# Ten joined pairs of p1 and p2, a re-ordered step list and 124 unread matmuls in a fused recurrence and rational feed-forward kernel

## The chip, the cores and the metric

The kernel runs on one core of one Trainium2 chip. The metric is the device time of one execution in microseconds (us), lower is better; a comparison goes by the median of several executions. Five engines work from instruction queues of their own, each strictly in order: TensorE (PE, with its weight loads shown as PEld), VectorE (DVE), ScalarE (ACT), GpSimd (POOL) and SyncE (SP, which here only issues DMAs).

## The reference

For 4 batches and 8 heads a state of 48 x 48 is decayed per row by a gate and receives an outer product at each of 768 steps; the query reads it. The heads' outputs, put side by side, go through a feed-forward layer whose activation is a rational function.

```python
# B, H, S, D = 4, 8, 768, 48
f = 1.0 / (1.0 + np.exp(-f_logit))
for t in range(S):
    state = f[:, :, t, :, None] * state + np.einsum('bhd,bhe->bhde', k[:, :, t], v[:, :, t])
    y[:, :, t] = np.einsum('bhd,bhde->bhe', q[:, :, t], state)
x = y.transpose(0, 2, 1, 3).reshape(B * S, H * D)          # 3072 x 384
h = x @ w_in                                               # 384 x 2048
P = a[0] + a[1] * h + a[2] * h**2 + a[3] * h**3
Q = 1.0 + np.abs(b[0]) * np.abs(h) + np.abs(b[1]) * h**2
out = (P / (Q + 1e-06)) @ w_out                            # 2048 x 384
```

## The kernel before

The work is cut into 12 units of 256 tokens; unit n is chunk n // 4 of batch n % 4, so that the state of a batch passes from unit n to unit n + 4. Within a unit the recurrence is done in two blocks of 128 tokens, by the chunked form: logarithms of the gates are summed over time with triangular matrices, q and k are scaled with the exponentials of those sums, and the output is a masked product inside the block plus a read of the state that enters it.

Every operation is a *step*, a short name with a unit and ranges, and one long string, `ORDER`, lists all steps. A loop at the end of the kernel calls them in that order; nothing else sets the order, so each engine executes its own steps in the order of the list. The steps:

- loads: `ld n f|q|k` on SP, `ld n v` on POOL; `wi` and `wo` load pieces of the two weights on POOL, `ab_` the coefficients. A pair of numbers after a load, as in `ld 0 f 2 4`, limits it to some of the head pairs 0 to 4. Constants: `ci` (identity), `cu 0` and `cu 1` (the triangular matrices Ui and Us), `cm`, `cz`; `fa`, `fb`, `fr` derive coefficients.
- gates: `ef` and `ls` on ACT (exponential, logarithm), `cs` on PE (the sums), `A` on ACT (exponential of the sums; `A n 0` for q, `A n 1` for k).
- recurrence: `xa n x` scales q (x = 0) or k (x = 1), on DVE or, with `p`, on POOL; `T` transposes the scaled q and k on PE; `Te` takes the result out of PSUM, on ACT with `s`, else on DVE; `sc n g` are the products of q and k on PE, `mk n g` masks them on DVE; `ic` and `si` build the next state on PE, `st n j` scales it on DVE; `yb` and `yi` form the output y on PE; `ye` evicts it as x. `vm` copies parts of v.
- feed-forward: `h n m0 m1` multiplies x with pieces m0 to m1 of the 16 column blocks of w_in (12 matmuls for four pieces); `hy` evicts them on ACT; then over halves `0 8` and `8 16` or the whole `0 16`: `sq` or `sa` (square, on DVE or ACT), `ab` (absolute value), `p1` and `p2` (two linear factors of P), `pm` (p1 times the square), `zv` on DVE or `zd` as an accumulating DMA (the denominator), `rq` (its reciprocal, ACT), `tv` or `ta` (the numerator, on DVE or as a DMA), `gm` (their product, DVE). `o n j m0 m1` multiplies with w_out, `oe` evicts, `so` stores.
- `tab` loads the activation table of the logarithm (0) or of the reciprocal (1).

`@0` to `@3` name one of four PSUM slots of two banks that a step opens; the slot is free again when the step that reads it is done, for example `hy` for `h`, `mk` for `sc`, `A` for `cs`, `st` for `ic`. `!m5` on a step and `^m5` on a later one on another queue make the later one wait for the first. Buffers rotate: one T and one masked product, two scaled q and k, three each of f, k, q, v, g and z, four x and hy.

Of the kernel before, what the change touches and what calls it, by code (L numbers as in the profile page):

```python
# [34 lines left out]
ye 2 s; ab 1 0 8; sc 3 0 @3; cs 5 @2; A 4 0; ab 0 0 8 !m8; xa 4 0 2 4 p ^m8; mk 3 0; A 4 1; ic 3 @1; sa 1 8 16
h 2 8 12 @0; st 3 0; ld 5 k; sq 0 0 8; si 3 1; h 2 12 16 @3; hy 2 8 12; pm 0 0 8 !m7; zd 0 0 8; ld 5 q
xa 4 1 2 4 p ^m7; ls 6; sc 3 1 @0; st 3 1 !m6; A 5 1; ld 6 k; vm 3 ^m6; mk 3 1; h 2 4 8 @1; ld 5 v; hy 2 12 16
xa 4 1 0 2; ef 7; yi 3 1 @0; xa 4 0 0 2; yb 3 0 2; wo 12 16; p1 1 8 16; hy 2 4 8; T 4 @3; wo 8 12
pm 1 8 16 !m10; A 5 0; ic 4 @1; wo 4 8; xa 5 1 0 2 p ^m10; si 4 0; Te 4 s; yb 3 2 4; st 4 0 !m11; ye 3 !m9
xa 5 1 2 4 p ^m11; si 4 1; sc 4 1 @2; h 2 0 4 @3; ld 7 k; mk 4 1; vm 4 ^m9; tab 1; rq 0 0 16; wo 0 4  # L40
sc 4 0 @0; p2 0 0 8 !m13; xa 5 0 2 4 p ^m13; yb 4 2 4 @2; st 4 1 !m12; xa 5 0 0 2 p ^m12; mk 4 0; si 5 0 @1
yi 4 0; ic 5; st 5 0; yb 4 0 2; tv 0 0 8 !m14; si 5 1; hy 2 0 4; h 3 4 8 @0; ld 6 q; ld 6 v ^m14; st 5 1
gm 0 0 8; yi 4 1; h 3 8 12 @3; zd 1 0 8; tab 0; ls 7; p1 1 0 8; h 3 12 16 @1; ye 4 s; gm 0 8 16; hy 3 4 8
zv 1 8 16; T 5 @2; hy 3 12 16; cs 6 @0; p1 2 8 16; Te 5 s; vm 5 v; o 0 0 12 16 @1; p2 1 0 16; hy 3 8 12
o 0 1 12 16; A 6 0; sc 5 0 @2; ab 2 0 8; cs 7 @3; A 6 1; pm 1 0 8; o 0 0 8 12; ef 8; sc 5 1 @0
xa 6 1 0 2 !m15; A 7 0; xa 6 1 2 4 p ^m15; o 0 1 4 8; mk 5 0 !m18; A 7 1; o 0 0 4 8; xa 7 1 0 2 p ^m18
sa 2 0 16; mk 5 1; h 3 0 4 @3; ta 1 8 16; sq 3 8 16; h 4 4 8 @2; p1 2 0 8; h 4 0 4 @0; tv 1 0 8; ls 8
zd 2 0 8; o 0 1 8 12; xa 6 0 2 4; hy 3 0 4; p2 2 0 8; o 0 1 0 4; hy 4 0 4; ab 2 8 16; yi 5 1 @3; yi 5 0
o 0 0 0 4; p2 2 8 16; hy 4 4 8; zd 2 8 16; ld 7 v ^m13; yb 5 0 2; pm 2 0 16 !m16; oe 0 0 2 s; yb 5 2 4
# [571 lines left out]
```

## Time and profile before

| | |
|---|---|
| median of three runs | 212.93 us (211.46 to 214.59) |
| profiled execution | 210.19 us, of which the span of instructions is 208.5 us |
| mean granted TensorE clock | 0.988 |
| busy: PE, DVE, ACT, POOL | 191.0, 187.0, 186.1, 77.8 us |
| matmuls, weight loads | 2894, 2894 |
| DMA | 43.15 MB, 207 GB/s in the mean |

The busy times are shares of the span; a row of a timeline gives the start, the duration, the engine, the line of the code, the operation with its tiles and shapes, and in brackets how long the engine stood idle before it and what ended that. A group of matmuls ends later than its last one starts by about a fifth of a microsecond.

### The profile page before, as it was taken

How to read it: one execution, taken by the hardware profiler on the slowest of the kernel's cores; microseconds unless marked ns; L12 is line 12 of the kernel's file. 1: busy time of each engine (PE TensorE's matmuls, PEld its weight loads, DVE VectorE, ACT ScalarE, POOL GpSimd, SP SyncE). 2: the span in 40 equal slices, each digit the busy share in tenths (PEclk: the TensorE clock that was granted, in tenths of full speed). 3: DMA queues.
4: the chain of work that ended last, by engine and by line, in shares of the span. 5: the costliest groups of instructions: out<-in, count | busy, mean ns of one | idle time of the engine just before them, and what ended most of it. 6: DMA issues, size and time to landing. Idle time of an engine off the chain costs nothing.

```text
span 208.5 us, 6605 instructions
## 1 busy us (share of the span) xinstructions
PE 191.0 (92%) x2894; PEld 139.4 (67%) x2894; DVE 187.0 (90%) x235; ACT 186.1 (89%) x172; POOL 77.8 (37%) x99
## 2 busy tenths in 40 slices
...
PEclk9999699999999999999999999999999999999998
...
GB/s 98 287 300 186 271 220 253 186 220 233 168 206 202 85 176 152 249 267 265 208 222 252 250 199 229 209 200 210 185 191 163 214 211 195 193 190 183 238 146 167
DMA packets 61820, 43.15 MB, mean 207 GB/s; under 512 B 51424, under 2 KB 56544, under 8 KB 61792
## 3 DMA queue, kind: packets, MB, share of 16 engines
...
q14 instruction: 6, 0.05, 0.1%
...
## 4 chain that ended last, share of the span: by engine, by line
PE 75%; DVE 10%; DMA 6%; SPq 4%; issue 2%; ACT 1%; DVEq 0%
PE op L549 31%; PE hp L469 26%; PE y L389 6%; SPq L209 4%; PE cs L304 3%; DMA v<-in_v_dram 3%; PE tp L345 3%; PE sc L368 2%; DMA q<-in_q_dram 2%; DVE scm L376 2%; DVE g L528 2%; PE sv L434 2%; DVE state L459 1%; PE sv L444 1%; DVE qkp L331 1%
## 5 line engine op out<-in xcount | busy, mean ns | idle before, releaser
L549 PE MATMUL op<-w_out_sb,g 128*128 128x384 bf16 x384 | 68.6, 326 | 0.0
L469 PE MATMUL hp<-x,w_in_sb 128*128 128x256 bf16 x576 | 68.0, 273 | 0.3 <-DVE state L459 0.3
L469 PEld LDWEIGHTS <-w_in_sb 128*128 128x128 bf16 x576 | 55.4, 98 | 9.4 <-issue 0.7
L549 PEld LDWEIGHTS <-g 128*128 128x128 bf16 x384 | 35.8, 98 | 22.6 <-DVE g L540 0.4
L481 ACT CAST hy<-hp 128x1024 bf16<-128x1024 f32 x48 | 47.8, 1027 | 2.6 <-PE hp L469 2.3
L508 ACT ACTIVATE z<-z 128x4096 bf16<-128x4096 bf16 (+1 forms) x16 | 44.5, 2780 | 1.1 <-DVE z L499 1.1
L540 DVE TENSOR_TENSOR g<-g,z 128x2048 bf16<-128x2048 bf16 (+2 forms) x24 | 28.9, 1218 | 1.1 <-issue 0.6
L503 POOL DMA_DIRECT2D z<-h x20 | 20.6, 1077 | 24.7 <-ACT h L490 17.0
L528 DVE TENSOR_TENSOR g<-g,h 128x2048 bf16<-128x2048 bf16 (+1 forms) x21 | 28.8, 1373 | 0.1
L376 DVE TENSOR_TENSOR scm<-sc,mask 128x1024 bf16<-128x1024 f32 x24 | 28.8, 1216 | 0.0
L490 ACT ACTIVATE h<-hy 128x2048 bf16<-128x2048 bf16 (+1 forms) x13 | 26.8, 2073 | 0.0
L326 ACT ACTIVATE A<-cs 128x768 f32<-128x768 f32 (+3 forms) x26 | 19.0, 779 | 6.5 <-PE cs L312 6.5
L532 POOL DMA_DIRECT2D g<-hy x15 | 13.8, 943 | 28.3 <-DVE g L528 9.3
L304 PE MATMUL cs<-lsp,Ui 128*128 128x384 bf16 (+1 forms) x39 | 12.0, 371 | 10.1 <-ACT lsp L294 8.7
L518 DVE TENSOR_SCALAR g<-hy,a_sb 128x2048 bf16<-128x2048 bf16 (+1 forms) x23 | 18.9, 829 | 1.4 <-ACT hy L481 1.4
L331 POOL TENSOR_TENSOR qkp<-k,A 128x384 bf16<-128x384 f32 x11 | 11.0, 1025 | 23.6 <-DVE g L540 10.4
L523 DVE TENSOR_SCALAR hy<-hy,a_sb 128x2048 bf16<-128x2048 bf16 (+1 forms) x20 | 18.3, 915 | 0.4
L209 POOL DMA_DIRECT2D v<-in_v_dram x12 | 12.1, 1012 | 15.7 <-DVE qkp L331 8.3
L494 DVE TENSOR_SCALAR z<-hy 128x2048 uint16<-128x2048 uint16 (+1 forms) x21 | 15.8, 764 | 0.0
L459 DVE TENSOR_TENSOR state<-sv,A 128x384 bf16<-128x384 f32 x20 | 11.0, 552 | 4.5 <-PE sv L444 2.4
L389 PE MATMUL y<-scm,v 64*32 64x128 bf16 x384 | 14.0, 218 | 0.8 <-DVE scm L376 0.7
L331 POOL TENSOR_TENSOR qkp<-q,A 128x384 bf16<-128x384 f32 x10 | 10.0, 1010 | 11.5 <-ACT A L326 5.5
...
## 6 DMA issues: line engine op xcount, KB each, us to landing
...
v<-in_v_dram POOLq DMA_DIRECT2D x12, 192.0 KB, 7.7
out_dram<-f SPq DMA_DIRECT2D x12, 192.0 KB, 3.9
out_dram<-osb SPq DMA_DIRECT2D x10, 192.0 KB, 6.4
```

Source lines behind the costliest of these rows:

```text
L209: return eng.dma_start(out=s[what][:, hh].rearrange("p h i d -> p h (i d)"), in_=src[s["b"], hh, t0:t0 + NT, :].rearrange("h (p i) d -> p ...
L331: i = (nc.gpsimd if eng == "p" else nc.vector).tensor_mul(s["qk"][:, x, :, hh, 0:D], s["qk"[x]][:, hh].rearrange("p h i d -> p i h d"), s[ ...
L376: return nc.vector.tensor_mul(t, s["sc", g].rearrange("s r a i t -> s (r a) (i t)"), mb)
L389: nc.tensor.matmul(s["y"][32 * a:32 * a + 32, j, kk * C:kk * C + C].rearrange("e (i t) -> e i t", i=2), lhsT, rhs, start=(j, a) not in s[" ...
L469: nc.tensor.matmul(t[:, m - m0, :].rearrange("f (j t) -> f j t", j=UB), w_in_sb[:, kk, m * P:(m + 1) * P], s["x"][:, :, kk, :], start=(kk ...
L481: nc.scalar.copy(fl(big(s, "hy"), m0, m1), fl(s["hp", m0], 0, m1 - m0))
L490: return nc.scalar.activation(fl(big(s, "h2"), m0, m1), fl(big(s, "hy"), m0, m1), AF.Square)
L503: return nc.gpsimd.dma_start(out=fl(big(s, "z"), m0, m1), in_=fl(big(s, "h2"), m0, m1), accum_op=ALU.add)
L508: return nc.scalar.add_instruction(mybir.InstActivation(name=nc.get_next_instruction_name(), func=AF.Reciprocal, ins=[nc.scalar.lower_ap(f ...
L528: return nc.vector.tensor_mul(fl(big(s, "g"), m0, m1), fl(big(s, "g"), m0, m1), fl(big(s, "h2"), m0, m1))
L540: return nc.vector.tensor_mul(fl(big(s, "g"), m0, m1), fl(big(s, "g"), m0, m1), fl(big(s, "z"), m0, m1))
L549: nc.tensor.matmul(s["op", g][:, j, 0:DM], big(s, "g")[:, m, C * j:C * j + C], w_out_sb[:, m, :], start=(s["on", j] == 1), stop=(s["on", j ...
```

## The change

Three things change, all in `ORDER` but for one new step.

- A new step `dn n w sl` opens a PSUM slot and issues n matmuls of Us with w times 64 columns of itself; nothing reads them. `dn 62 1` stands ahead of `cs 0` and `dn 62 2` between `cs 0` and `cs 1`.
- Where both halves of a unit went through `p1` or `p2` in two instructions, more of them now go through one. Joined now: `p1` of units 2, 3, 4 and 10 (6 stays so) and `p2` of units 2, 4 and 8 (7 and 10 stay so); taken apart: `p2` of units 1 and 3. In the same way `pm` of 6 and 7 and `gm` of 2 and 6 are joined, `pm` of 2 and 5, `gm` of 4 and 7, `ab` of 6, 7 and 9, and the DVE products `xa 8 0` and `xa 10 1` are taken apart, and `rq` of 6 and 7 on ACT.
- All other steps are the same, in another order: mostly a few places off. `Te 0 0 2` moves from ACT to DVE, `xa 2 0 0 2` from POOL to DVE, `oe 11 0 1` from ACT to DVE. In the head, the loads, the constants, the gates and the products of units 0 to 2 stand in another order.

The first lines of the list before and after, and the new step:

```diff
-cu 1; cz 1; ld 0 f 2 4; ld 0 v; ab_ b s; cz 3; cz 0; ld 0 f 0 2; ci; ld 0 q 2 4; ld 1 f; cu 0; ld 0 k 0 2
-ef 0 2 4; ls 0 2 4; cm; ld 0 k 2 4; cz 2; fa; cs 0 2 4 @0; ef 0 0 2; ls 0 0 2; ld 0 q 0 2; cs 0 0 2 @1; ld 1 k
-A 0 1 0 2; A 0 1 2 4; A 0 0 2 4; A 0 0 0 2; fr; ld 2 f; ef 1; xa 0 1 2 4; ls 1; xa 0 0 2 4; vm 0 v; cs 1 @2
-xa 0 0 0 2; ld 1 q; xa 0 1 0 2 !m0; ld 1 v ^m0; ld 3 f; ic 0 @3; wi 2 8 16; A 1 1; wi 3 8 16; A 1 0
-T 0 0 2 @0; st 0 0; ld 2 q; ab_ a s; wi 1 8 16; xa 1 1 2 4; T 0 2 4 @1; wi 0 8 16; Te 0 0 2 s; sc 0 0 @2
-xa 1 0 0 2; Te 0 2 4 s; xa 1 0 2 4; ef 2; si 0 1; sc 0 1 @0; xa 1 1 0 2; st 0 1; T 1 @1; mk 0 0; ld 2 k
-mk 0 1; yb 0 0 2 @3; yi 0 1; Te 1; ef 3; yb 0 2 4; ic 1 @2; ls 2; st 1 0 !m1; sc 1 1 @0; ld 2 v ^m1; ye 0 s
-cs 2 @1; mk 1 1 !m4; ls 3; sc 1 0 @3; wi 0 0 8; A 2 0; si 1 1; ld 5 f; cs 3 @0; wi 3 0 8; st 1 1; A 2 1
-vm 1 v !m2; wi 2 0 8; mk 1 0; xa 2 0 0 2 p ^m2; A 3 0; h 0 8 12 @2; wi 1 0 8; xa 2 0 2 4; h 0 12 16 @1
-hy 0 8 12; fb; ld 4 f; yb 1 0 2 @3; hy 0 12 16; yb 1 2 4; xa 2 1; yi 1 1; ye 1 s; p1 0 8 16; T 2 @2
-A 3 1; ab 0 8 16; h 1 12 16 @1; Te 2 s; sq 0 8 16; h 1 8 12 @3; p2 0 8 16; hy 1 12 16; pm 0 8 16 !m3; ld 3 q
-ic 2 @0; hy 1 8 12; vm 2 ^m3; sc 2 1 @2; st 2 0; sc 2 0 @1; mk 2 1; ld 3 k; si 2 1; ef 5; h 0 0 4 @3; st 2 1
-ls 5; ld 6 f; ab 1 8 16; h 0 4 8 @2; ef 4; tv 0 8 16 !m5; hy 0 0 4; ld 4 k; xa 3 0 2 4 p ^m5; h 1 4 8 @0
-mk 2 0; ls 4; ld 4 q; ld 3 v ^m4; hy 0 4 8; h 1 0 4 @3; xa 3 1; ld 4 v; hy 1 4 8; xa 3 0 0 2; yb 2 0 2 @1
...
+ci; ld 0 f 0 2; cu 1; ld 0 f 2 4; ld 0 q 0 2; ld 0 v; ab_ b s; ld 1 f; cu 0; ld 0 k 0 2; ef 0 0 2; ls 0 0 2
+cm; ef 0 2 4; cz 1; ld 0 k 2 4; ls 0 2 4; cz 0; ld 0 q 2 4; cz 2; cz 3; dn 62 1 @3; cs 0 2 4 @0; cs 0 0 2 @1; dn 62 2 @2; ld 1 q
+vm 0 v; A 0 0 0 2; A 0 0 2 4; xa 0 0 0 2; ef 1; ld 1 k; fa; A 0 1 2 4; A 0 1 0 2; ls 1; xa 0 1 2 4; ld 2 f
+xa 0 1 0 2; cs 1 @2; xa 0 0 2 4 !m0; ld 1 v ^m0; ld 3 f; ic 0 @3; wi 3 8 16; A 1 1; wi 0 8 16; ld 2 q; ab_ a s
+A 1 0; T 0 0 2 @0; st 0 0; wi 1 8 16; xa 1 1 2 4; T 0 2 4 @1; wi 2 8 16; Te 0 0 2; xa 1 0 2 4; sc 0 0 @2
+Te 0 2 4 s; xa 1 1 0 2; si 0 1; ef 2; sc 0 1 @0; xa 1 0 0 2; ld 2 k; mk 0 0; fr; T 1 @1; mk 0 1; yb 0 0 2 @2
+ef 3; yi 0 1; Te 1; ls 3; yb 0 2 4; ic 1 @0; ls 2; st 0 1; sc 1 1 @1; ye 0 s; st 1 0 !m1; ld 2 v ^m1
+sc 1 0 @3; mk 1 1; cs 3 @2; wi 1 0 8; mk 1 0; cs 2 @1; ld 5 f; wi 0 0 8; wi 3 0 8; si 1 1; A 2 0; st 1 1
+wi 2 0 8; h 0 8 12 @3; vm 1 v; A 2 1; fb; A 3 0; xa 2 0 2 4; h 0 12 16 @0; xa 2 0 0 2; hy 0 8 12; ld 4 f
+yb 1 0 2 @1; hy 0 12 16; yi 1 1; xa 2 1; yb 1 2 4; ye 1 s; sq 0 8 16; T 2 @3; A 3 1; h 1 12 16 @0; ab 0 8 16
+Te 2 s; p1 0 8 16; h 1 8 12 @1; p2 0 8 16; hy 1 12 16; pm 0 8 16; ld 3 q; ic 2 @2; hy 1 8 12; sc 2 1 @3
+st 2 0 !m2; ld 3 k; vm 2 ^m2; sc 2 0 @0; mk 2 1; si 2 1; ef 5; h 0 0 4 @1; ls 5; ab 1 8 16 !m3; ld 6 f
+ld 3 v ^m3; h 0 4 8 @3; st 2 1; ef 4; tv 0 8 16 !m4; hy 0 0 4; ld 4 q; xa 3 0 2 4 p ^m4; h 1 4 8 @2; mk 2 0
+ls 4; ld 4 v; hy 0 4 8; h 1 0 4 @1; xa 3 0 0 2; xa 3 1; ld 4 k; hy 1 4 8; yi 2 1 @0; p1 0 0 8; T 3 @3
...
@@ -461,6 +461,13 @@
             s["sv"][:, j].rearrange("p (b w) (r d) -> p b (w r) d", b=2, r=2),
             _at(s["ae"], [[DM + 16 if n else DM // 2 + 8, 2], [1, 4], [0, D]], 4 * j))
 
+    def dn(n, w, sl):
+
+        t = slot(sl, [P, 2, 512], F32, "dn")
+        for i in range(n):
+            nc.tensor.matmul(t[:, i % 2, 0:w * R].rearrange("p (w c) -> p w c", c=R), Us,
+                             _at(Us, [[0, w], [1, R]]), start=True, stop=True)
+
     def h(n, m0, m1, sl):
         s = unit(n)
         t = s["hp", m0] = slot(sl, [P, 4, NT], F32, "hp")
@@ -573,7 +580,7 @@
                           reason="begins behind it")
 
     steps = dict(ld=load, wi=load_w_in, wo=load_w_out, ab_=load_ab, cu=const_u, ci=const_i, cm=const_m,
-                 cz=const_z, fa=coef_a, fb=coef_b, fr=coef_r, tab=tab, ef=ef, ls=ls, cs=cs, A=A, xa=xa, T=T, Te=Te,
+                 cz=const_z, fa=coef_a, fb=coef_b, fr=coef_r, tab=tab, ef=ef, ls=ls, cs=cs, dn=dn, A=A, xa=xa, T=T, Te=Te,
                  sc=sc, mk=mk, vm=vm, yi=yi, yb=yb, ic=ic, si=si, ye=ye, st=st, h=h, hy=hy, sq=sq, sa=sa, ab=ab,
                  zv=zv, zd=zd, rq=rq, p1=p1, p2=p2, pm=pm, ta=ta, tv=tv, gm=gm, o=o, oe=oe, so=store)
     for step in ORDER.replace("\n", ";").split(";"):
```

More of the change, by code (lines that the diff above doesn't have):

```diff
@@ L35 @@
[L35 to L49, printed above, removed]
@@ new lines @@
+xa 6 1 2 4 p ^m12; o 0 0 12 16; sa 2 0 16; mk 5 1; o 0 1 4 8; o 0 1 8 12; xa 6 1 0 2; sc 5 0 @3; vm 5 v
+p2 1 0 8 !m16; h 4 0 4 @1; xa 7 1 0 2 p ^m16; mk 5 0; o 0 0 0 4; ef 8; tv 1 0 8; zd 2 8 16; o 0 0 4 8
+hy 4 0 4; zd 2 0 8; o 0 1 0 4; pm 2 0 8; hy 3 0 4; ic 6 @3; o 0 0 8 12; ls 8; p2 2 0 16; yb 5 2 4 @1
+oe 0 0 2 s; yi 5 0; yi 5 1; pm 2 8 16 !m13; yb 5 0 2; so 0 0 2; ta 2 0 8; xa 6 0 0 2 p ^m13; si 6 0
+h 4 12 16 @0; ye 5 !m24; ld 7 q; tab 1; rq 1 0 16; ld 7 v ^m15; ld 8 q; st 6 0; h 4 8 12 @2; xa 6 0 2 4
@@ new lines @@
+o 2 0 8 12; zd 3 8 16; xa 7 0 2 4; yi 6 0 @3; o 2 0 12 16; pm 4 8 16; ld 10 q; si 7 0 @1; yb 6 0 2; A 8 0
+ld 9 q; p2 3 8 16; ic 7; sa 3 0 8; h 5 0 4 @2; xa 8 0 0 2; st 7 0; xa 8 0 2 4; yi 6 1; hy 5 0 4; si 7 1
+ab 3 0 8; yb 6 2 4; st 7 1; o 2 1 0 4; ef 9; zd 3 0 8; pm 3 8 16; o 2 0 4 8; ye 6 s; T 7 @2; p2 3 0 8; ls 9
+o 2 1 4 8; pm 4 0 8; ef 10; cs 9 @1; oe 2 0 2 s; pm 3 0 8; h 6 12 16 @3; Te 7 s; so 2 0 2; vm 7 v
+ab 4 0 8 !m19; A 9 0; ta 3 0 8; xa 8 1 2 4 p ^m19; sc 7 0 @0; ld 10 k; hy 6 12 16; h 5 4 8 @2; mk 7 0
```

107 lines of the change are left out of this document (56 added, 51 removed).

## The prediction

> **What bounds the kernel now.** I read the page first, then busy time by stage (cut where the timeline changes character), then the timeline of the head.
>
> ```profile
> span 208.5 us, 6605 instructions
> PEclk9999699999999999999999999999999999999998
> ```
> ```profile
> 10.60:15.50 4.90, 4.90 (x63) 3.64 (x62) 3.58 (x10) 2.72 (x5) 3.04 (x5) 1.00 1.10 300
> ...
> 20.83:22.19 1.36, 0.00 (x1) 0.03 (x1) 1.36 (x2) 0.16 (x1) 0.81 (x1) 1.00 1.13 219
> 22.19:26.00 3.81, 3.81 (x45) 2.31 (x45) 1.36 (x4) 1.52 (x2) 2.28 (x5) 0.55 1.25 291
> ...
> 30.80:45.25 14.45, 14.13 (x259) 11.46 (x256) 14.41 (x18) 13.89 (x17) 3.38 (x5) 1.00 1.01 222
> 45.25:50.00 4.75, 3.84 (x59) 3.18 (x59) 4.27 (x6) 4.26 (x5) 2.06 (x3) 1.00 1.25 230
> 50.00:64.20 14.20, 13.65 (x309) 10.55 (x309) 13.99 (x18) 14.00 (x13) 11.54 (x14) 1.00 1.21 193
> 64.20:204.20 140.00, 139.93 (x1890) 99.23 (x1887) 136.19 (x147) 135.16 (x113) 50.30 (x55) 1.00 1.03 203
> ```
>
> Columns: window, its length, busy time (instructions) of PE, PEld, DVE, ACT, POOL, granted clock, DMA share, GB/s. From 64.2 to 204.2 us PE is busy 139.93 of 140.00 us; DVE has 3.8 us and ACT 4.8 us to spare. So the second half runs at PE's pace, and its length can change only by the count of PE instructions and by switches between kinds. What can move the end is when PE gets into that state. Before 64.2 it loses time: 1.36 us at 20.83, half clock to 26.0 (mean 0.55), and 0.32 + 0.91 + 0.55 = 1.78 us idle from 30.8 to 64.2. The profiled execution took 210.19 us: 208.5 of span and 1.7 around it. The median of the three runs is 212.93, so 2.74 us lie between them that this trace does not show. I work in the profile's time and add the difference of the sum to 212.93. About 2% (4.3 us) is what a measurement of this kernel can tell from no change.
>
> The head as it stands:
>
> ```profile
> 1.45 0.30 POOL L232 TENSOR_SCALAR_AFFINE_SELECT Us<-Us 128x128 bf16<-128x128 bf16 x1
> 7.28 1.67 ACT L326 ACTIVATE A<-cs 128x384 f32<-128x384 f32 x4 [1.02 <-PE cs L312]
> 9.70 0.84 ACT L294 ACTIVATE lsp<-f 128x768 bf16<-128x768 f32 x1
> 10.05 0.56 DVE L331 TENSOR_TENSOR qkp<-k,A 128x384 bf16<-128x384 f32 x1 [3.42 <-DMA k<-in_k_dram]
> 10.60 0.48 PE L304 MATMUL cs<-lsp,Ui 128*128 128x384 bf16 x1 [3.35 <-ACT lsp L294]
> 11.93 0.35 PE L312 MATMUL cs<-ind,lsp 128*128 128x4 bf16 x8
> 12.46 0.92 POOL L209 DMA_DIRECT2D v<-in_v_dram  x1 [8.25 <-DVE qkp L331]
> 12.96 1.89 PE L345 MATMUL tp<-ident,qkp 128*128 128x128 bf16 x16
> 13.37 2.22 POOL L215 DMA_DIRECT2D w_in_sb<-in_moe_w_in_dram  x4
> 14.49 1.03 DVE L331 TENSOR_TENSOR qkp<-q,A 128x384 bf16<-128x384 f32 x2 [0.39 <-DMA q<-in_q_dram]
> 16.11 1.07 PE L345 MATMUL tp<-ident,qkp 128*128 128x128 bf16 x16
> 18.67 1.22 DVE L356 COPY T<-tp 128x2048 bf16<-128x2048 bf16 x1
> 22.19 0.32 PE L304 MATMUL cs<-lsp,Ui 128*128 128x384 bf16 x1 [1.36 <-issue]
> 24.66 0.56 DVE L459 TENSOR_TENSOR state<-sv,A 128x384 bf16<-128x384 f32 x1 [2.45 <-PE sv L444]
> 26.00 2.78 PE L469 MATMUL hp<-x,w_in_sb 128*128 128x256 bf16 x24
> ```
>
> PE waits for `ls 1` (3.35 us before 10.60), DVE for k until 10.05 and for q of unit 1 until 14.49: to 16 us the head runs at the pace of the loads. Then DVE works through two masks, `Te 1` (18.67 to 19.89), a state and a mask. `cs 2` at 22.19 comes after 1.36 us with no wait that the profile shows; DVE idles 2.45 us for the state behind it (24.66), and the first `h` of unit 0 cannot begin until 26.00, since `cs 2`, `sc 1 0`, `si 1 1` and `cs 3` are ahead of it on PE at the low clock. The clock is read from the rows: 16 transposes of 128 columns take 1.89 us at 12.96 and 1.07 us at 16.11, some 107 and 57 ns apart once the last one's latency of about 0.2 us is taken off, although the column says 1.00 in both. So PE is at half rate until 14.85 at least, and at full rate by 16.11.
>
> **The change part by part.**
>
> *The dummies.* `dn 62 1` is 62 matmuls of 64 columns, `dn 62 2` 62 of 128. They read Us, which two instructions for `ident` now precede on POOL: 1.75 us (row at 1.45) plus about 0.55, an estimate from its neighbours, gives 2.3 us. At half rate a 128-column one costs 107 ns, so a 64-column one 53 ns if its weight load is hidden, 62 x 53 = 3.3 us, ending at 5.6. Other bound: eight pairs of load and 4-column matmul at 11.93 take 0.35 us, 44 ns each; added in full it is 62 x 97 = 6.0 us, ending at 8.3. I take the first, since the transposes too load 128 columns each and still run at their streaming rate. The load of `f` for the second half is now issued second instead of fourth, so both `ls 0` should be done by about 5.6 too; `cs 0` then takes until 6.6 to 7.4, against 7.28 where A starts today: nothing gained, nothing lost. `dn 62 2` follows: 3.5 us at full rate, 6.6 us at half; from 7.0 it ends at 10.5 or 13.6. `cs 1` is next on PE, and its input is ready at 9.70 + 0.84 = 10.54. So at full rate the block just fits into the idle 3.35 us and costs nothing; without that cover it costs up to 3.1 us. I take full rate: by then PE has worked from 2.3 to 7 us nearly without a break, and today it is at full rate by 16.11, at most 5.5 us after its work began at 10.60.
>
> [...]
>
> *The head's order.* q of unit 1 is issued ahead of k 1 and f 2, and q of unit 0 is split the other way. DVE does one of four products before k lands; at 10.05 two remain on k, then one on the late q. `ic 0` can start near 11.5 instead of 12.2, and `cs 1` with its successors run at full clock. But k 1 now comes behind q 1 (row at 14.49), as many bytes later; unit 1's products begin near 13.2 instead of 13.55, and `Te 0 0 2`, moved from ACT to DVE, takes 0.6 of that back (half of the 1.22 of `Te 1`). So T 1 and the first mask stay near 16.0: 0 us, bounds -0.5 and +0.5.
>
> *From 16 to 26 us.* `cs 2` and `si 1 1` now stand behind `sc 1 0` and `cs 3`, and `st 0 1` behind `Te 1`. What frees the PSUM slot of `h 0 8 12` is DVE's chain: two masks, `Te 1`, two states, two masks, at 1.14 us a mask or copy (both last 1.22, the mask by its row below; neighbours overlap by some 0.08: two masks and Te 1 fill 3.5 us up to 19.89) and 0.47 a state. From 16.0 that is 4 x 1.14 + 1.14 + 2 x 0.47 = 6.6, so 22.7; with 0.4 for the waits of a semaphore chain, 23.1. The weights must be there as well: today's four issues run from 13.37 to 15.6, and w_in takes 8.2 us to land, 23 to 24; they go out about 0.5 earlier behind v 1 (12.46 today, behind DVE's last product). So `h 0` begins at 23.1 instead of 26.0: **-2.9 us**, bounds -1.5 (weights late, the 1.36 us stall kept) and -3.4. Both losses are in it: the stall lies under the wait for the mask, and the low clock no longer slows work that is on the path. DVE's `xa 2 0 0 2`, taken from POOL, fills 0.55 us of a DVE that waits for `hy` there.
>
> ```profile
> w_in_sb<-in_moe_w_in_dram POOLq DMA_DIRECT2D x8, 192.0 KB, 8.2
> ```
>
> *From 26 to 64 us.*
>
> ```profile
> 39.28 1.80 POOL L209 DMA_DIRECT2D v<-in_v_dram  x2
> 45.88 0.51 PE L434 MATMUL sv<-v,qkp 64*128 64x96 bf16 x16 [0.63 <-DMA v<-in_v_dram]
> ```
>
> `ic 3` waits 0.63 us for v 3, which POOL issues only at 39.28, behind `xa 3 0 2 4`. In the new order v 3 goes first, so that wait and the DVE state behind it fall away. Of the 1.78 us of idle PE I count 1.6 as gone: **-1.6 us**, bounds -1.8 and +1.0 (new waits of the same size as the old).
>
> *Joins and splits.*
>
> ```profile
> L518 DVE TENSOR_SCALAR g<-hy,a_sb 128x2048 bf16<-128x2048 bf16 x22 | 17.6, 805 | 1.4 <-ACT hy L481 1.4
> L518 DVE TENSOR_SCALAR g<-hy,a_sb 128x4096 bf16<-128x4096 bf16 x1 | 1.3, 1343 | 0.0
> L523 DVE TENSOR_SCALAR hy<-hy,a_sb 128x2048 bf16<-128x2048 bf16 x16 | 12.9, 809 | 0.3
> L523 DVE TENSOR_SCALAR hy<-hy,a_sb 128x4096 bf16<-128x4096 bf16 x4 | 5.4, 1338 | 0.1
> L528 DVE TENSOR_TENSOR g<-g,h 128x2048 bf16<-128x2048 bf16 x18 | 22.0, 1221 | 0.1
> L528 DVE TENSOR_TENSOR g<-g,h 128x4096 bf16<-128x4096 bf16 x3 | 6.9, 2286 | 0.0
> L508 ACT ACTIVATE z<-z 128x4096 bf16<-128x4096 bf16 x8 | 29.1, 3640 | 0.0
> L508 ACT ACTIVATE z<-z 128x2048 bf16<-128x2048 bf16 x8 | 15.4, 1921 | 1.1 <-DVE z L499 1.1
> L376 DVE TENSOR_TENSOR scm<-sc,mask 128x1024 bf16<-128x1024 f32 x24 | 28.8, 1216 | 0.0
> ```
>
> A joined p1 saves 2 x 0.805 - 1.343 = 0.27 us, a p2 0.28. Counted in the lists, seven such pairs are joined and two taken apart: 5 x 0.27 = 1.4 us less. Of pm, gm, ab and the unit 8 and 10 xa, four pairs are joined and nine taken apart, each about 2 x 1.221 - 2.286 = 0.16: 0.8 us more. DVE gains 0.6 us net over the run, gives 0.55 to xa 2 and 0.6 to Te 0, and takes one 0.45 us eviction at the end. Two `rq` split on ACT cost 2 x (2 x 1.921 - 3.640) = 0.4 us, less the 0.58 that left it. None of this is on PE's path after 64 us; it changes the 3.8 and 4.8 us of slack by less than 1: 0 us.
>
> *Other steps a few places off.* PE's list after the head has the same instructions. Two lines of the chain that ended last show what a switch costs, four `o` ahead of a small group and four ahead of `h`-like work:
>
> ```profile
> 135.17 0.76 PE op L549 x4
> 137.23 0.65 PE op L549 x4
> ```
>
> Counting neighbours in the list, `o` is followed by a small group (sc, y, cs, ic) 23 times instead of 19, and y begins 27 runs instead of 23. At 0.1 us for a switch out of `o` at most, and part of it lost in waits anyway: **+0.2 us**, bounds 0 and +0.8. The last units keep their form (`o 11 1` ends, eviction, two stores): 0 us, but `ta 11 8 16` has one step less between it and its `gm`, so up to +1.5.
>
> Sum: -2.9 - 1.6 + 0.2 = **-4.3 us**: 205.9 us for a profiled run, 212.93 - 4.3 = **208.6 us** for the median.
>
> **The rivals.**
>
> 1. *The gain is given back.* DVE or ACT takes PE's place. After 64.2 they have 3.8 and 4.8 us of slack, and they too start earlier, so for it one must stay late, as when `cs 2` still stalls 1.36 us and k 2 or w_in land late. Then only about 1 us is left: 212 us.
>
> 2. *More than forecast.* The 2.74 us by which the median is above the profile are losses of the same head in other runs (another phase of the clock, later loads), and go as well: 208.6 - 2.7 = 205.9. For it: loads set the head's pace and they vary. Against it: no trace shows those runs.
>
> 3. *The dummies hold up PE.* PE takes its list in order, so `cs 1`, `ic 0`, T 0 and all of unit 1 wait behind `dn 62 2`. If the first block takes its long bound (to 8.3), `cs 0` ends near 9.6, A starts 2.3 us late, and the second block at half rate ends at 16.2 where `cs 1` was ready at 10.54: 5.7 us late. The stall taken away gives 1.4 back: +4.3, 217.2 us. It decides from the point where the block ends after about 12 us. Against it: the transposes' rate, and the early work that raises the clock.
>
> 4. *The dummies do not raise the clock.* Then the second block at half rate ends at 13.6 instead of 10.5: 3.1 us of the 4.3 go, 211.7 us.
>
> **How the numbers follow.** The forecast (gain carried to the end, 207 to 210.3) gets 0.53; 0.30 of it lies under 208.67, which is 2% off. Rival 1 gets 0.09, rival 2 0.13, rival 3 0.20, rival 4 0.05. Faster by over 2%: 0.30 + 0.13 = 0.43. Slower by over 2% (above 217.2): nearly all of rival 3, whose price is the bound itself and to which the +1.0 and +1.5 of new waits would add, 0.19. Within 2%: the other 0.38. The range runs from 205.0, rival 2 with most of the larger bound of the head, to 218.0, rival 3 with part of those waits; some 0.05 lies below and 0.12 above. The forecast's own range is 207 to 210.3.
>
> **What would show it.** Right: 16 transposes of T 0 in about 1.07 us; `cs 1` at 10.6 to 11.0; no PE idle of 1.4 us near 21; first `h` near 23; no wait of `ic 3` for v; PE busy without gaps from about 60. Wrong: `cs 1` after 12 us, a granted clock of 0.5 after 16 us, or PE idle after 64 us in tenths of a microsecond per unit, which would mean that the steps a few places off, held here at 0.2, matter more than the head.

## The result, and the profile after

The changed kernel takes 213.43 us in the median of 23 runs (210.86 to 218.54), the kernel before 211.17 us (208.31 to 216.01); the ratio is 1.0124, 95% interval 1.0092 to 1.0156. It is slower by some 2.5 us, where 4.3 us less was forecast. Ratios compare the runs of each kernel that are within 1.5% of its fastest, and the profiled run of the changed kernel (217.15 us) is one of its longest, so its trace is read below beside others of the same list.

Lines of the page of after, with the number of instructions, the granted clock and the queue that carries code:

```profile
span 215.4 us, 6863 instructions
...
PEclk9996999999999999999997999999999999999999
...
q8 instruction: 23, 0.38, 0.6%
```

Busy time by stage, after (window, length, busy time and instructions of PE, PEld, DVE, ACT, POOL, granted clock, DMA share, GB/s):

```profile
10.60:15.50 4.90, 2.64 (x49) 2.04 (x46) 3.35 (x10) 2.45 (x4) 2.30 (x4) 1.00 0.91 239
15.50:20.00 4.50, 4.13 (x93) 3.25 (x93) 3.98 (x6) 3.17 (x5) 0.85 (x2) 0.66 1.34 205
20.00:25.24 5.24, 4.28 (x118) 2.91 (x111) 4.42 (x5) 1.44 (x3) 2.47 (x4) 0.97 1.14 248
25.24:47.30 22.06, 21.66 (x406) 18.16 (x406) 21.05 (x30) 21.49 (x25) 4.87 (x7) 1.00 1.21 243
47.30:67.00 19.70, 17.65 (x376) 13.61 (x374) 18.72 (x23) 18.46 (x19) 13.50 (x16) 1.00 1.18 197
67.00:100.00 33.00, 33.00 (x495) 23.10 (x493) 32.63 (x37) 32.56 (x27) 10.50 (x12) 1.00 1.02 194
100.00:140.00 40.00, 35.56 (x526) 25.92 (x525) 34.29 (x38) 33.49 (x33) 16.28 (x19) 0.96 1.00 187
140.00:205.00 65.00, 65.00 (x799) 45.14 (x798) 63.89 (x66) 63.79 (x49) 26.73 (x25) 1.00 1.02 197
```

The gap-free state that the kernel before keeps from 64.2 us on is broken: PE is idle for 4.44 us between 100 and 140 us, and for 2.05 between 47.3 and 67. Rows of PE's timeline, after (start, duration, step, and in brackets the idle time before it and what ended that):

```profile
2.31 3.49 PE L468 MATMUL dn<-Us 128*128 128x64 bf16 x62 [2.31 <-POOL Us L232]
...
7.13 3.62 PE L468 MATMUL dn<-Us 128*128 128x128 bf16 x62
11.58 0.32 PE L304 MATMUL cs<-lsp,Ui 128*128 128x384 bf16 x1 [0.83 <-ACT lsp L294]
...
13.00 1.07 PE L345 MATMUL tp<-ident,qkp 128*128 128x128 bf16 x16
15.87 0.42 PE L368 MATMUL sc<-T 48*64 48x128 bf16 x16 [1.80 <-DVE T L356]
...
16.90 1.89 PE L345 MATMUL tp<-ident,qkp 128*128 128x128 bf16 x16
...
22.91 0.36 PE L368 MATMUL sc<-T 48*64 48x128 bf16 x12 [0.59 <-issue]
...
25.24 2.78 PE L476 MATMUL hp<-x,w_in_sb 128*128 128x256 bf16 x24
...
58.05 0.52 PE L434 MATMUL sv<-v,qkp 64*128 64x96 bf16 x16 [0.81 <-DMA v<-in_v_dram]
...
115.21 1.68 PE L476 MATMUL hp<-x,w_in_sb 128*128 128x256 bf16 x10 [2.03 <-issue]
124.80 0.82 PE L556 MATMUL op<-w_out_sb,g 128*128 128x384 bf16 x4 [1.27 <-DVE g L547]
...
130.55 0.29 PE L389 MATMUL y<-scm,vmp 64*32 64x128 bf16 x8 [0.89 <-POOL vmp L383]
```

The dummies run as priced and end at 10.75, ahead of `cs 1`. T 0 goes at full rate (1.07), but behind a gap of 1.80 the granted clock falls to 0.50 (16.93 to 20.34): T 1 takes 1.89. The first `h` begins at 25.24 instead of 26.00, not at 23.1. Two of the rows end with "issue", that is, with nothing that the profile shows, and both lie inside a run of equal matmuls: between the 20th and 21st of 32 products `sc`, and in the middle of `h`. A third such gap, of 0.41 us, ends at 62.52, also in an `h`.

To compare orders I counted matmuls in each trace. Behind each step named below both lists have issued the same set of PE steps, so the time from one to the next is the same work (us, from the start of the first `h` of unit 0 to the start of the first matmul behind each step; the last column ends with the start of the last matmul).

```
                     h 0 at  to h 2 0 4  to ic 6  to T 7  to h 7 8 12  to yb 9 2 4  to o 7 1 0 4  to the last
before                 26.0     30.6      22.2     23.5      25.9          11.5          38.2         25.9
e4_before_dummies      25.2     30.9      22.2     23.5      25.9          11.8          38.2         25.9
after                  25.2     30.2      23.5     23.7      32.8          11.7          38.0         25.9
a_again                27.3     31.1      23.0     23.7      28.3          11.7          38.0         25.9
a_shift                25.6     30.2      22.9     24.0      26.9          11.7          38.0         25.9
a_shift_again          24.8     31.5      22.3     23.8      27.0          11.7          38.0         25.9
```

### The profile page after: what moved, and what is told of

Read it like the earlier page. It is cut to its first block, busy times and chain, and to the rows that moved or that the text cites. A ratio compares the mean times of both kernels' runs of the same rounds, so it can differ in the third digit from the quotient of the medians.

```text
span 215.4 us, 6863 instructions
## 1 busy us (share of the span) xinstructions
PE 198.6 (92%) x3018; PEld 145.8 (68%) x3018; DVE 190.0 (88%) x238; ACT 185.6 (86%) x172; POOL 80.8 (37%) x98
## 4 chain that ended last, share of the span: by engine, by line
PE 55%; DMA 15%; DVE 15%; SPq 4%; issue 4%; ACT 2%; POOL 1%; POOLq 0%; DVEq 0%; ACTq 0%
PE op L556 25%; PE hp L476 17%; DMA q<-in_q_dram 9%; PE y L389 4%; DMA v<-in_v_dram 4%; SPq L209 3%; DMA k<-in_k_dram 3%; PE tp L345 3%; DVE g L525 2%; DVE scm L376 2%; PE sc L368 2%; DVE z L501 2%; DVE h L492 2%; PE cs L304 2%; ACT A L326 1%
## 5 line engine op out<-in xcount | busy, mean ns | idle before, releaser
L476 PE MATMUL hp<-x,w_in_sb 128*128 128x256 bf16 x576 | 68.9, 275 | 2.4 <-issue 2.4
L515 ACT ACTIVATE z<-z 128x2048 bf16<-128x2048 bf16 (+1 forms) x18 | 44.9, 2503 | 1.2 <-DVE z L506 1.2
L510 POOL DMA_DIRECT2D z<-h x20 | 21.7, 1227 | 22.9 <-ACT h L497 11.4
L539 POOL DMA_DIRECT2D g<-hy x15 | 16.8, 1146 | 28.5 <-DVE g L535 8.7
L331 POOL TENSOR_TENSOR qkp<-k,A 128x384 bf16<-128x384 f32 x11 | 11.7, 1125 | 22.2 <-DVE g L525 11.2
L501 DVE TENSOR_SCALAR z<-hy 128x2048 uint16<-128x2048 uint16 x24 | 16.8, 703 | 0.0
L331 POOL TENSOR_TENSOR qkp<-q,A 128x384 bf16<-128x384 f32 x9 | 9.4, 1054 | 16.6 <-DMA q<-in_q_dram 8.5
L389 PE MATMUL y<-scm,v 64*32 64x128 bf16 x384 | 14.6, 223 | 0.2 <-DVE scm L376 0.2
L345 PE MATMUL tp<-ident,qkp 128*128 128x128 bf16 x192 | 14.4, 235 | 0.0
L345 PEld LDWEIGHTS <-qkp 128*128 128x128 bf16 x192 | 12.9, 106 | 1.0
```

The lines of the kernel that those rows point to most:

```text
L345: nc.tensor.transpose(t[:, x, i, p, :], s["qk"][:, x, i, 2 * p:2 * p + 2, :].rearrange("t h d -> t (h d)"), ident)
L389: nc.tensor.matmul(s["y"][32 * a:32 * a + 32, j, kk * C:kk * C + C].rearrange("e (i t) -> e i t", i=2), lhsT, rhs, start=(j, a) not in s[" ...
L476: nc.tensor.matmul(t[:, m - m0, :].rearrange("f (j t) -> f j t", j=UB), w_in_sb[:, kk, m * P:(m + 1) * P], s["x"][:, :, kk, :], start=(kk ...
L510: return nc.gpsimd.dma_start(out=fl(big(s, "z"), m0, m1), in_=fl(big(s, "h2"), m0, m1), accum_op=ALU.add)
L515: return nc.scalar.add_instruction(mybir.InstActivation(name=nc.get_next_instruction_name(), func=AF.Reciprocal, ins=[nc.scalar.lower_ap(f ...
```

## The experiments

**Late q 9 and the dummies.** In after's trace DVE waits 4.92 us at 115.66 for q of unit 9, which is issued later than before; this was the first suspect (theory L).

```profile
115.66 0.56 DVE L331 TENSOR_TENSOR qkp<-q,A 128x384 bf16<-128x384 f32 x1 [4.92 <-DMA q<-in_q_dram]
```

Two kernels move that load, two take the dummies out of the new list (theory D: they delay the head) or put them into the old one; theory J blames the joins:

```diff
 # e1_after_q9_early                        # e3_before_q9_late
-ld 9 q; p2 3 8 16                         -o 1 0 12 16; ld 9 q
+p2 3 8 16                                 +o 1 0 12 16
-tv 2 8 16; si 6 1                         -yb 6 2 4 @3; ld 10 f
+ld 9 q; tv 2 8 16; si 6 1                 +yb 6 2 4 @3; ld 10 f; ld 9 q
 # e2_after_no_dummies                      # e4_before_dummies
-dn 62 1 @3; cs 0 2 4 @0                   -cs 0 2 4 @0
+cs 0 2 4 @0                               +dn 62 1 @3; cs 0 2 4 @0
-cs 0 0 2 @1; dn 62 2 @2; ld 1 q           -cs 0 0 2 @1; ld 1 k
+cs 0 0 2 @1; ld 1 q                       +cs 0 0 2 @1; dn 62 2 @2; ld 1 k
```

> The changed kernel with one step moved: the load of q for unit 9 goes out behind the load of q 8, as soon as its buffer is free (about 80 us), instead of behind q 10 at 96 us. Theory L (the late q 9 is the loss): DVE's wait of 4.9 us for q near 110 us and the 4.4 us of idle PE from 100 to 140 us go, and the time falls from 1.012 of the kernel before to 0.995 to 1.000. Theory D (the dummies delay the head) and theory J (the joins and the new neighbours on PE cost it): the ratio stays at 1.010 to 1.015.

> The changed kernel without its two blocks of unread matmuls. Theory D: 2 us better, ratio 1.000 to 1.004 of the kernel before. Theory L: the wait near 110 us stays, ratio 1.010 to 1.016; the first matmuls of unit 0 run at half rate again, which costs 0 to 0.8 us, since loads set the pace there.

> The kernel before with the load of q for unit 9 moved from ahead of q 8 to behind f 10, where it goes out at about 96 us as in the changed kernel. Theory L: DVE waits for it near 105 to 110 us, PE idles 1 to 4 us there, ratio 1.005 to 1.02. Theories D and J: no change, 0.997 to 1.003.

> The kernel before with only the two blocks of unread matmuls added, at the same places between the same steps. Theory D: 1.008 to 1.015. Theory L: 0.996 to 1.003, with the transposes of unit 0 at full rate (16 in 1.07 us instead of 1.89) and nothing gained by the end, as DVE still waits for k and q.

Measured: e1 1.0156 (1.0084 to 1.0228), e3 0.9993 (0.9947 to 1.0038), e4 0.9981 (0.9939 to 1.0023); e2 has no ratio, and a median of 217.67 us (213.01 to 221.28) against 210.37 for before on that chip. So the late q is not the cause: in e1 its wait is gone, and the two gaps without a wait are larger than in after (e3 says less, since in its trace DVE does not wait for the late q at all):

```profile
24.53 0.36 PE L368 MATMUL sc<-T 48*64 48x128 bf16 x12 [2.50 <-issue]
```

```profile
118.58 1.27 PE L476 MATMUL hp<-x,w_in_sb 128*128 128x256 bf16 x10 [2.59 <-issue]
```

The dummies are not what makes the new list slow: without them its fastest run, 213.01 us, is still above the median of before. What they are worth there is not shown, since e2's runs lie too far apart; in the old list they bring nothing to the end. In e4 the clock is full from 6.7 us on (T 0 takes 1.07), and yet `h` of unit 0 begins only at 25.19, because the weights were not there:

```profile
25.19 2.78 PE L476 MATMUL hp<-x,w_in_sb 128*128 128x256 bf16 x24 [1.21 <-DMA w_in_sb<-in_moe_w_in_dram]
```

**Where in the list.** Both lists have issued the same steps at a few places, so the new list can be followed to such a place and the old one from there (or the reverse), with the PSUM slots renamed at the seam; b_join has only the seven joins that the change makes.

```diff
 # h1: new list up to xa 3 0 0 2 (48 us), then the old one; h2: the reverse, without dn
 # h3: new up to rq 0 0 16 (66 us); h5: up to ta 4 8 16 (115 us); h6: up to p2 6 8 16 (143 us)
 # b_join, p1 of 2, 3, 4, 10 and p2 of 2, 4, 8 in the old list, for instance
-p1 3 8 16; ... p1 3 0 8
+p1 3 0 16; ...
```

> The new list up to the first products of unit 3 (about 48 us: dummies, order of the head, Te 0 0 2 on DVE, xa 2 0 0 2 on DVE, k of unit 1 behind q of unit 1, v of unit 3 ahead of the POOL product), then the old list to the end; the PSUM slots are renamed at the seam. Theory H (the head costs the time): as the changed kernel, some 2 to 3 us above before (1.010 to 1.015). Theory R (the order behind the head costs it): at or under before, 0.993 to 1.000, since the changed kernel began h of unit 0 at 25.24 instead of 26.00 in its profile, and v of unit 3 is early. Theory F (PE stands without instructions at a block boundary of its code wherever some 250 short instructions pass in 5 to 6 us): the boundaries stand at the same counts as in the changed kernel, so one stall of 0.8 to 2.5 us near 23 to 25 us, none after 100 us where the old order has its long stretches of h and o: 1.000 to 1.008.

> The complement: the old list up to the first products of unit 3 (no dummies), then the new list. Theory H: as before, 1.000. Theory R: slower by the whole loss and by the gain of the head that is missing, 1.012 to 1.020, with PE idle of 4 us or more between 100 and 140 us as in the changed kernel's profile. Theory F: the boundaries stand 8 instructions from those of the changed kernel, so the stall near 113 to 115 us stays: 1.005 to 1.012.

> The new list up to the first reciprocal (about 66 us), then the old list. In the changed kernel's profile PE is idle 2.05 us between 47.3 and 67 us, in before 0.82 us between 48 and 64.2 us. Theory R with the loss after 100 us: equal to the kernel with the new list to 48 us, plus at most 1.2 us. If the loss lies in 48 to 66 us (v of unit 4 issued late on POOL, one state waits 0.81 us for it): 1 to 1.5 us above that kernel. Theory H: 1.010 to 1.015 in both.

> The kernel before with the seven joins of p1 (units 2, 3, 4, 10) and p2 (units 2, 4, 8) that the change has, at the place of one of the halves, and nothing else changed. The prediction's working: DVE saves 7 x 0.275 = 1.9 us of busy time that PE hides: 1.000, 0.995 to 1.003. Theory J (a joined instruction holds back what reads its first half, so the joins cost): 1.008 or more.

> The new list up to ta of unit 4 and T of unit 8 (about 115 us; the joins of p1 of units 2 to 4 and p2 of units 2 and 4 in it), then the old one. The new list to 66 us gave 1.0039, all of it 1.0124. If the loss comes in units 5 to 8 before 115 us: 1.009 to 1.014. If it comes behind 115 us: 1.003 to 1.006.

> The new list up to T of unit 10 (about 143 us), then the old one. If the loss comes between 115 and 143 us, where the profile of the changed kernel shows PE waiting for g (1.27 us) and for a copy of v (0.89 us): 1.009 to 1.014, and the kernel that changes back at 115 us at 1.003 to 1.006. If it comes behind 143 us, in the last units and the end: 1.003 to 1.006.

Measured: h1 1.0039 (1.0001 to 1.0077), h3 1.0039 (1.0005 to 1.0074), b_join 1.0003 (0.9962 to 1.0043), h2 1.0254 (1.0178 to 1.0330), h5 1.0160 (1.0091 to 1.0229), h6 1.0219 (1.0133 to 1.0305). The joins cost nothing. The new list to 48 us, whose head alone was to bring 2.9 us, costs 0.4%, and in h1's trace one place stands out:

```profile
20.74 0.47 PE L364 MATMUL sc<-T 48*64 48x128 bf16 x20
23.45 0.54 PE L364 MATMUL sc<-T 48*64 48x128 bf16 x12 [2.24 <-issue]
```

The same step, the same 20 of 32, as in after and e1. The stretch from 66 to 115 us adds the next part. h2 and h6 say less: their seams make waits of their own (2.56 us for v 3 in h2, 2.0 us for `hy` in h6), which neither list has.

**Where PE's code ends.** Counting PE's loads and matmuls, the gaps without a wait begin behind instruction 446 in before, behind 702, 2234 and 3768 in after and e1 (some of these in the hybrids with dummies), and behind 1978 and 3512 in e2: 184 to 190 above a multiple of 256 each time. 702 is 446 plus the 248 of the dummies, but for 8, and without the dummies the last two gaps stand 256 earlier, not 248. The page's row for code has 23 packets, 0.38 MB together; in the trace each has 16384 bytes, and there is one for every 262 of the 6036 PE instructions. The theory (F) that fits these counts: code comes in blocks of 256 instructions, and PE stands where a block is used up before the next is there, for 2.24 us in h1 and up to 2.59 in e1.

The times of the code packets in the traces bear the theory out. Put in order, the n-th packet belongs to the n-th of these places in PE's code. All 22 gaps of more than 0.15 us without a wait end 1.3 to 1.6 us behind the end of their packet, and at none of the 434 such places in the 20 traces (taken at 192 above a multiple of 256) does PE go on sooner than 1.29 us behind it. In before the packet lies at 19.84 to 20.77 and PE goes on at 22.19; in after another lies at 112.91 to 113.80 and PE goes on at 115.21. A packet starts between 2.2 us ahead of PE's passing the place before and 6.8 us behind it, in the median 2.7 behind; for the packets of the gaps it is 3.2 to 6.5.

The gap of before is also in the other old lists without dummies: 2.73 us in b_switch, 1.41 in e3 and 0.85 in b_join. In the last two the profile names a logarithm on ACT, which had ended 0.8 and 0.4 us earlier; the packets had ended 1.41 and 1.46 us earlier.

```profile
22.43 0.48 PE L304 MATMUL cs<-lsp,Ui 128*128 128x384 bf16 x1 [1.41 <-ACT lsp L294]
```

As a further test, the same columns of dummies go into half as many instructions, so that every later step stands 124 instructions further ahead in the code:

```diff
 # a_shift, a_shift_again (after), h1_shift (h1); a_again is after itself
-dn 62 1 @3; ... dn 62 2 @2
+dn 31 2 @3; ... dn 31 4 @2
 # a_shift_v5: also
-xa 4 0 2 4 p ^m6
+xa 4 0 2 4 p ^m6; ld 5 v
 # b_dn_v3: e4, and
-ef 4; tv 0 8 16 !m5
+ef 4; ld 3 v ^m4; tv 0 8 16 !m5
```

> The changed kernel with the same columns of dummies in half as many instructions: 31 of 128 and 31 of 256 columns instead of 62 of 64 and 62 of 128, so everything behind them stands 124 instructions (62 loads and 62 matmuls) earlier in TensorE's code, at the same place of the work. Theory F (TensorE's code comes in blocks of 256 instructions, and it stands still where a block is used up before the next is there): the idle time without a wait moves away from the 20th of the 32 products sc of unit 1 (near 23 us) and from the middle of the h near 115 us; the first goes, since its block boundary now falls among cs and h, where PE waits for other things, and the time is below the changed kernel's: 1.000 to 1.009 against before. Rival (the idle time belongs to those steps, through a wait that the profile does not show): both stalls stay at the same steps, ratio 1.010 to 1.015.

> The new list to 48 us, then the old one (1.0039 before), with the same halving of the dummies' count. Theory F: the stall of 2.2 us behind the 20th sc of unit 1 goes, h of unit 0 begins at 25.0 to 25.5 instead of 27.16 us, held by w_in, and the ratio falls to 0.993 to 0.999. Rival: stall and ratio stay, 1.002 to 1.006.

> The changed kernel itself, on one chip with the two that follow. Its time is 1.010 to 1.015 of before. Theory F: where its profile is one of the longer runs, the idle time without a wait stands near 115 us and is followed by a stretch of half clock; where it is one of the shorter runs, the products up to T of unit 8 (115 us in before) are done by 117 us and no such stretch follows.

> The changed kernel with 31 dummies of 128 and 31 of 256 columns, on the same chip as the changed kernel. Theory F: 1.0 to 2.5 us below it (1.002 to 1.008 of before), with no idle time without a wait over 1 us. Rival: the same time as the changed kernel within 0.6 us; then the moved stalls cost nothing in the end, and the loss is in the order of the steps alone.

> As the kernel before it in this list, with the load of v of unit 5 ahead of the zd of unit 0 on POOL (issued near 46 instead of 50.35 us). If the wait of ic 5 for that v (0.8 to 0.9 us near 58 us in three profiles of the new order) sets the end: 0.6 to 1.0 us below the kernel before it. If the gain of the early units is given back by the next resource, as the new list to 48 and to 66 us suggested: within 0.4 us of it.

> The kernel before with the two blocks of dummies of the change and with v of unit 3 issued ahead of the POOL product of unit 3, as the change has it. With the dummies alone the ratio was 0.998, h of unit 0 began at 25.2 instead of 26.0 us, and ic 3 waited 0.96 us for v 3. If PE sets the pace from there on, both gains reach the end: 0.990 to 0.995. If DVE and the loads take its place: 0.996 to 1.000.

On one chip a_again took 214.58 us in the median (211.20 to 216.54) and a_shift_again 211.15 (210.41 to 211.92), with before at 209.72; five of six runs of the first are above all runs of the second. The ratios, 1.0187 (1.0109 to 1.0264) and 1.0123 (1.0081 to 1.0164), overlap. a_shift had 1.0104 (1.0064 to 1.0144), with a median of 211.57 against 210.54; after's 1.0124 lies inside that. So the ratios do not show how much time the moved gaps give back, and both shifted kernels are above what theory F expected. The timelines, a_again first, show the gap go from between the 20th and 21st `sc`:

```profile
20.54 0.71 PE L368 MATMUL sc<-T 48*64 48x128 bf16 x20
23.44 0.54 PE L368 MATMUL sc<-T 48*64 48x128 bf16 x12 [2.19 <-issue]
23.91 0.50 PE L304 MATMUL cs<-lsp,Ui 128*128 128x384 bf16 x1
...
27.30 1.06 PE L476 MATMUL hp<-x,w_in_sb 128*128 128x256 bf16 x4
```

```profile
20.12 0.64 PE L368 MATMUL sc<-T 48*64 48x128 bf16 x32
20.70 0.34 PE L304 MATMUL cs<-lsp,Ui 128*128 128x384 bf16 x1
...
24.76 3.41 PE L476 MATMUL hp<-x,w_in_sb 128*128 128x256 bf16 x16 [1.55 <-DMA w_in_sb<-in_moe_w_in_dram]
```

In a_shift_again the 32 products run in one piece, and what holds `h` is the weights. In a_again the gap is paid twice, since the clock falls behind it (a `cs` of 384 columns takes 0.50 for 0.34, and `h` begins 2.5 us later). Windows of a_again, the gap and the stretch behind it:

```profile
20.54:23.44 2.90, 0.66 (x20) 0.41 (x21) 2.00 (x3) 0.30 (x1) 1.74 (x3) 0.86 1.12 220
23.44:27.30 3.86, 3.86 (x42) 2.17 (x43) 1.22 (x1) 0.10 (x1) 1.41 (x3) 0.50 1.41 264
```

Neither a_shift nor a_shift_again has a gap that ends with "issue" in its list of waits. h1_shift has 1.0011 (0.9966 to 1.0056) for h1's 1.0039: the gap at `sc` is gone and `h` begins at 25.86 instead of 27.16, but the intervals overlap, and a gap of 1.2 us has come up inside y near 60 us, behind instruction 1978, again 186 above a multiple of 256 (as the gap of `ic 5` in the next kernel is 187). That the gaps follow the place in the code and not the step is shown by this, and by the packets' times. Why a packet starts late, whether because loads keep the DMA engines busy or for another reason, is not shown.

a_shift_v5 is at 1.0177 (1.0105 to 1.0250) and 211.82 us: the wait of `ic 5` for v is gone, but the same `ic 5` now has a gap of 0.8 us without a wait, and `ic 1` waits 1.19 us for its own v in that trace; nothing is gained. b_dn_v3 is at 1.0030 (0.9998 to 1.0061): the two real gains of the change in the old list bring nothing. `h` of unit 0 begins at 24.72, the wait for v 3 is gone, and then `h` waits for the other half of the weights:

```profile
24.72 2.78 PE L476 MATMUL hp<-x,w_in_sb 128*128 128x256 bf16 x24 [0.82 <-DMA w_in_sb<-in_moe_w_in_dram]
...
35.44 5.40 PE L476 MATMUL hp<-x,w_in_sb 128*128 128x256 bf16 x48 [1.48 <-DMA w_in_sb<-in_moe_w_in_dram]
```

**What is left without the gaps.** a_shift is still above before. From `ic 6` to the end the old order takes 125.0 us, a_shift and a_shift_again 126.5 and 126.4; most of it, 1.1 and 1.2, lies between T 7 and `h 7 8 12`, where PE changes kind of matmul 27 times instead of 18 (theory S: each change has a price). The last two kernels change that number (161 in both lists):

```diff
 # b_switch: 171, one o moved between two pieces of y or two sc, for instance
-yi 6 0; zd 3 0 8; ld 8 v; pm 3 0 8; yb 6 0 2; o 2 0 0 4
+yi 6 0; o 2 0 0 4; zd 3 0 8; ld 8 v; pm 3 0 8; yb 6 0 2
 # a_shift_group: 151, units 7 and 8 of a_shift in larger pieces, for instance
-sc 8 0 @2; zd 5 8 16; xa 9 1 0 2 p ^m21; o 3 1 12 16
+o 3 1 12 16; sc 8 0 @2; zd 5 8 16; xa 9 1 0 2 p ^m21
```

> The kernel before with ten more changes between kinds of matmul on TensorE (171 for 161 in its list), made in units 6 to 11 by moving one o between two products sc, or between two pieces of y; the work is the same. Theory S (each such change costs TensorE some 0.15 us, read from the stretch between T of unit 7 and h 7 8 12, where the new list has 27 changes for 18 and takes 1.4 us longer with PE busy throughout): 1.5 us longer, ratio 1.005 to 1.009, and each piece between the same two counts of matmuls longer by 0.15 us per change. The prediction's price (0.1 us at most for a change out of o): under 1 us, 1.000 to 1.004.

> The changed kernel with 31 dummies of 128 and 31 of 256 columns, and in units 7 and 8 ten changes between kinds of matmul fewer (151 for 161): products sc of one unit side by side, y of one unit in one piece, the o of unit 3 together, as the old list mostly has them. Theory S: 1.4 us below the kernel with the old places (211.15 to 211.57 in two measurements), 209.7 to 210.2, ratio 1.000 to 1.004, and the stretch from T of unit 7 to h 7 8 12, 27.2 us in a_shift, 25.8 us as in before. Rival (what PE loses there is set by DVE and the loads, not by the changes): the stretch stays at 27 us or PE idles in it instead, and the ratio at 1.007 to 1.012.

b_switch: 1.0114 (1.0066 to 1.0162), 213.22 us against 211.70. Its stretches grow where the changes were put: `ic 6` to T 7 by 0.6 us for four, of which PE is idle 0.2; T 7 to `h 7 8 12` by 0.2 for two; from there to `yb 9 2 4` by 1.0 for one, of which PE is idle 0.9 for a mask; to `o 7 1 0 4` by 0.2 for three. Without the idle time that is 0.9 us for ten, 0.1 us each: the prediction's price, not theory S's 0.15. The ratio is above what that price gives. The profiled run, the longest of the six, is 2.9 us late already at `ic 6`, ahead of all changes, with its gap of 2.73 us at `cs 2`; what the rest of the ratio comes from stays open.

a_shift_group: 1.0004 (0.9965 to 1.0042), 211.84 us against 211.70. The ratio is as theory S wanted, the stretch is not: T 7 to `h 7 8 12` takes 27.6 us instead of 27.0, and PE now waits in it:

```profile
110.38 0.24 PE L389 MATMUL y<-scm,v 64*32 64x128 bf16 x4 [1.01 <-DVE scm L376]
```

The same stretch, T 7 to `h 7 8 12`, in before, a_shift, a_shift_again and a_shift_group (length, then busy time of PE, PEld, DVE, ACT, POOL):

```profile
102.32:128.19 25.87, 25.87 (x452) 20.14 (x450) 25.21 (x28) 25.81 (x26) 10.76 (x12) 1.00 1.19 227
102.72:129.65 26.93, 26.48 (x451) 20.29 (x449) 26.27 (x30) 26.26 (x26) 12.82 (x14) 1.00 1.18 196
102.35:129.39 27.04, 26.30 (x451) 20.25 (x450) 26.12 (x30) 26.24 (x26) 12.34 (x14) 1.00 1.18 201
102.75:130.34 27.59, 26.09 (x451) 20.48 (x450) 25.62 (x30) 26.29 (x26) 12.80 (x14) 1.00 1.09 185
```

Theory S took PE as busy throughout, and it was not: of the 1.1 and 1.2 us, 0.45 and 0.74 are idle time, mostly for v of unit 8. The other 0.6 and 0.4 are busy time, and nine changes can have no more than that: a_shift_group, with 17 changes where before has 18, is still busy 0.2 us longer than before. Its idle time, for late masks above all, takes more than the ten changes save. Why its ratio is lower than a_shift's all the same, its one trace does not show.

## Why the prediction was wrong

- **The dummies: right.** 3.49 and 3.62 us for 3.3 and 3.5; `cs 0` was not late, the block ended before `cs 1`, rival 3 did not come. `cs 1` began at 11.58, not 10.6 to 11.0, because `ls 1` ended later; that is outside what was to show it right.
- **The head, -2.9 us: wrong, and the main failure.** h 0 began at 25.2, 27.3, 25.6 and 24.8 in four traces of the new list, for 26.0 before and 23.1 forecast. Two steps of the working failed. "The stall lies under the wait for the mask" treated the 1.36 us of before as a fixed slack; it is a place in the code, it stayed 20 products into the `sc` of unit 1 in the lists with 124 dummies and took 0.59 to 2.50 us. And the weights, put at 23 to 24, came at 24.7 to 26.5 in the five traces where w_in held `h` (in e4 and a_shift_again for 1.21 and 1.55 us). So the bound of -3.4 was out of reach, and no more than 1.3 us was to be had. No run shows the 0.4 us taken for the waits of a semaphore chain: in before's trace y starts at 18.77, 0.05 us behind the masks that it waits for, and a state at 20.52, 0.04 behind the end of its `ic`.
- **The order of the head, 0 us within 0.5:** `Te 0 0 2` on DVE behind a product that waits for k held `sc 0 0` for 1.80 us in after (0.72, 0.72 and 1.17 in a_shift, a_shift_again and a_again). T 1 came at 16.90 instead of 16.11, 0.8 us where the bound had 0.5; in a_shift and a_shift_again it came at 16.25 and 15.96, inside it.
- **26 to 64 us, -1.6: wrong.** The wait for v 3 went, as argued (0.18 for 0.63). But from h 0 to `h 2 0 4` the new order took 30.2 to 31.5 us instead of 30.6, and to `ic 6` 22.3 to 23.5 instead of 22.2, where v 5 came 0.81 late in after. The sum is +0.3 to +1.2 in the four traces: new waits, and in two of them the half clock (16 matmuls of `h` took 3.41 us in a_shift_again and 4 took 1.06 in a_again, where 24 take 2.78 at full rate), took the place of the old waits; the bounds (-1.8 to +1.0) had allowed for new waits and the value taken had not.
- **Joins and splits, 0: right.** DVE's rows have 1343 ns for a joined p1 as in before, and b_join 1.0003.
- **Other steps a few places off, +0.2 within 0 to 0.8: mis-sized.** From `ic 6` on it is +1.5 and +1.4 in the two traces without gaps, and nothing behind `h 7 8 12`. The price of a change of kind, 0.1 us at most, was right as far as b_switch's trace tells. The count of all changes is equal in both lists, so a net count said nothing: nine more fell between T 7 and `h 7 8 12`, and the term left out that v came late there, for which PE stood most of 0.45 and 0.74 us.
- **What no step had:** the gaps at such places of PE's code (22 of more than 0.15 us at the 434 places of the 20 traces), and the half clock behind some of them (0.50 from 23.44 to 27.30 in a_again, and from 115.91 to 119.33 in after). Between the medians of a_again and a_shift_again lie 3.4 us, though their ratios overlap. "PE idle after 64 us" was named as what would prove the forecast wrong, and it did.
- **The sum.** In a_shift, without gaps, the terms are -0.4 for the head, +0.3 to `ic 6` and +1.5 behind it, about +1.5 us in all, for -2.9, -1.6 and +0.2. So the gaps alone do not explain the failure.
- **Rival 1**, the gain given back, was the nearest: its 212 us lie within the runs of the changed kernel, and its reason, a stall at 21 us that stays and weights that come late, was the right one for the head. It had 0.09. Rival 2 rested on a median 2.74 us above the profiled run; over 23 runs before's median is 211.17, 1.0 above it.

No version here is shown to be faster than before (the nearest are e4 with 0.9981, e3 with 0.9993 and b_join with 1.0003).
